# Rows normalised on GpSimd by adding a negated mean, and an instruction emitter with other costs and settings

## The chip, the cores and the metric

The kernel runs on one core of a Trainium2 chip. The metric is the device time of one execution in microseconds. The engines are named as in the profile: PE (TensorE matmul) and PEld (its weight loads), DVE (VectorE), ACT (ScalarE), POOL (GpSimd) and SP (SyncE, which here only issues transfers).

## What is computed

Two transformer layers on x of 2048 rows by 512 columns, in bfloat16. Each layer is attention with 32 heads of width 16, and a gated feed-forward part with 1792 hidden columns. Cut to what matters:

```python
def _A_ref(x, wqkv, wo):
    q, k, v = split(x @ wqkv)                       # 32 heads of 16 columns
    scores = jnp.einsum("bhqd,bhkd->bhqk", q, k) * (Dh ** -0.5)
    p = _softmax(scores, axis=-1)
    o = jnp.einsum("bhqk,bhkd->bhqd", p, v)
    return o_as_rows @ wo

def _B_ref(x, w_gate, w_up, w_down):
    return (_gelu(x @ w_gate) * (x @ w_up)) @ w_down

x = x + _A_ref(_layernorm(x), A_wqkv, A_wo)
x = x + _B_ref(_layernorm(x), B_w_gate, B_w_up, B_w_down)
x = x + _A_ref(_layernorm(x), A_wqkv, A_wo)         # the same weights again
x = x + _B_ref(_layernorm(x), B_w_gate, B_w_up, B_w_down)
```

`_layernorm` subtracts the mean of a row and divides by the root of its variance plus 1e-5.

## The kernel before

The work that takes the time is the exponential of the scores: 2 layers x 32 heads x 2048 x 2048. A tile is 128 keys by 512 queries of one head. Four heads make a group and lie 32 partitions apart; eight groups and four blocks of 512 queries make 32 units a layer, each of 64 tiles, so there are 4096 tiles. For each tile PE multiplies keys by queries (line 1392), an engine takes the exponential, and PE multiplies the result with V (line 1538); V has a column of ones, which gives the row sums as well. Products with V of four heads run side by side in PE.

Two engines share the exponentials. ScalarE takes groups of three and of two PSUM banks in turn, one instruction for each (line 1406), and writes fPT. VectorE takes single tiles by another way: it turns scores into the bits of a float16 by adding a bias and storing as int16 (line 1446, into fPI), and then makes three shifted copies of up to four such tiles at once (line 1486, into fPP), so that a sum of four approximations is taken. Each VectorE tile thus needs four products with V, where one of ScalarE needs one.

The order of all instructions is fixed before the kernel runs, by an emitter inside the kernel's own Python. It keeps a modelled clock for each engine. Every instruction has a written cost, and `_Sched.op` places it where its engine and its inputs are free by that clock. The main loop at the end of `_emit_fast` asks, at each moment that PE is free in the model: are banks free for the next scores (`fill`)? If not, is there time before they are for products with V (`pv`), for a piece of the feed-forward part or a projection (`Piece`), or for filler[...] (`keep_clock`, line 1558, a product with zeros)? VectorE, GpSimd and transfer jobs are taken from queues by `pump_one`, by modelled start time and priority. On the chip each engine runs its own list in that order, held by semaphores alone: where a written cost is wrong, an engine waits in front of an instruction that the model thought ready.

`vector_tile` decides whether the next slot of scores brings a tile for VectorE. It adds up the modelled work that stands before VectorE and says yes while this is less than `DVE_LATE`. `behind` and `pace` hold VectorE tiles back while a feed-forward part lags.

After attention on a block of queries, `post` runs its output projection (line 640 with fWO), adds x (line 1055), and normalises the rows in `ln_thread`: statistics on VectorE (lines 587 and 588), for two rows of tiles at a time the factor on GpSimd in `ln_scale` (lines 594 and 596), the rows themselves in `ln_apply` (line 606), and a transposing transfer (`turn`, line 288) into fXNT. Then come the gate and up products (line 1070) and the down products (line 1134). A row of tiles is normalised on GpSimd in all blocks but the last of a layer, 36 in all; the others go to VectorE. `ln_apply` with `eng` "pool" and with `eng` "dve" is the same instruction before the change: subtract the mean, multiply by the factor.

The very last block is cut into two halves of 256 queries, so that little is left after the last exponential.

Of the kernel before, what the change touches and what calls it, by code (L numbers as in the profile page):

```python
# [11 lines left out]
ALU = mybir.AluOpType  # L12
ACTF = mybir.ActivationFunctionType
AX = mybir.AxisListType
AP = bass.AP
# [160 lines left out]
def _emit_fast(nc, es, x_in, wqkv, wo, wg, wu, wd, out, n_rep=2):  # L176
# [10 lines left out]
    F = wg.shape[1]  # L187
# [10 lines left out]
    VW = 17  # L198
    NPH = 4
    NPART = 6  # L200
    DVE_LATE = 2.0
    WAIT_D = 0.45
    OCT = 1024.0
    LOG2E = 1.4426950408889634
# [23 lines left out]
    CM05 = sb("fCM05", [128, 4], F32)  # L228
    QMASK = sb("fQMASK", [128, 2], F32)
    ZV = sb("fZV", [128, VW], F16)  # L230
    NPT = 7
    PT = sb("fPT", [128, NPT, 1536], BF)
# [5 lines left out]
    Q = sb("fQ", [128, NQS, 512], F16)  # L238
# [21 lines left out]
    sch = _Sched()  # L260
# [22 lines left out]
    def turn(grp, dst, src, r, w):  # L283
        if grp not in sch.groups:
            sch.add_dma_group(grp, serial=True)
        t = max(sch.free["sp"], sch.ready("sp", r, w)) + 1.0
        wire[0] = max(t, wire[0]) + 128 / 180.0
        return sch.op("sp", lambda e: e.dma_start_transpose(dst, src), r=r, w=w, grp=grp, cost=1.0,
                      lat=wire[0] - t + 1.6)

    SW, MM = 0.107, 0.216
    HAM, LEAST, BACK = 3.413, 0.425, 0.425
# [8 lines left out]
    def change(kind):  # L301
        return SW if kind_now[0] != kind else 0.0
# [164 lines left out]
    def job(eng, prio, ops, then=None, ported=False):  # L467

        serial[0] += 1
        jobs[eng].append((prio, serial[0], ops, then, ported or eng == "pool"))  # L470
# [109 lines left out]
    def xn(i, alt):  # L580
        return HT[:, i + 4 * alt, 0:D].bitcast(F16)
# [5 lines left out]
        dve(prio, [(lambda e: e.bn_stats(ST[:, i, :], rows), [key], [("ST", i)], 0.72),  # L587
                   (lambda e: e.bn_aggr(MV[:, i, :], ST[:, i, :]), [("ST", i)], [("MV", i)], 0.1)], then)

    def ln_scale(n, then, lo=0):  # L590
        keys = [("MV", lo + i) for i in range(n)]
        var = AP(MV, 2 * lo + 1, [[16, 128], [2, n]])
        job("pool", 1, [
            (lambda e: e.tensor_scalar(LNS[:, 0, lo:lo + n], var, LN_EPS, None, op0=ALU.add), keys,
             [("LNS", lo + i) for i in range(n)], 0.25),
            (lambda e: e.tensor_tensor(LNS[:, 1, lo:lo + n], LNS[:, 0, lo:lo + n], CM05[:, 0:n], op=ALU.pow),
             [("LNS", lo + i) for i in range(n)] + [("CM05",)], [("LNS", lo + i) for i in range(n)], 0.45 + 0.16 * n)], then)

    def ln_check(n, lo=0):
        var = AP(MV, 2 * lo + 1, [[16, 128], [2, n]])  # L600
# [1 line left out]
                 [("MV", lo + i) for i in range(n)] + [("OKV",)], [("OKV",)], 0.1)])  # L602

    def ln_apply(i, rows, key, eng, alt, then=None, us=None, st=0):
        us = us or (1.05 if eng == "pool" else 0.46)
        job(eng, 1, [(lambda e: e.tensor_scalar(xn(i, alt), rows, MV[:, st + i, 0:1], LNS[:, 1, st + i:st + i + 1],  # L606
                                                op0=ALU.subtract, op1=ALU.mult),
                      [key, ("LNS", st + i), ("MV", st + i)], [xnkey(i, alt)], us)], then, ported=True)

    def transpose_piece(i, tt, alt=False, eng="dve", then=None):  # L610
# [65 lines left out]
    def qproj(layer, up):  # L676

        qb, c = min(up // NCK, NQB - 1), up % NCK
        h = up // NCK - (NQB - 1) if layer == n_rep - 1 and NQB > 1 and up // NCK >= NQB - 1 else None
        q0, qn = (0, 512) if h is None else (256 * h, 256)  # L680

        def evac(b):
            ops = []
            for p in range(2):
                slot = (layer * NU + 2 * up + p) % NQS
                ops.append((lambda e, p=p, slot=slot: e.tensor_scalar(Q[:, slot, q0:q0 + qn], bank(b)[:, 0:qn],
                                                                     QMASK[:, p:p + 1], None, op0=ALU.mult),
                            [BK[b], ("QMASK",)], [("Q", slot)], 0.086 + 0.001042 * qn))
            evac_job(1, b, ops, got((layer, "q", up)))
        lo = 512 * qb + q0  # L690
        return mm_piece([(WQ[:, ck, 128 * c:128 * (c + 1)], XNT[:, ck, lo:lo + qn]) for ck in range(NCK)],
                        [("XNT", t) for t in range(lo // 128, (lo + qn) // 128)] + [("WQ", c)], evac, cols=qn)
# [312 lines left out]
    def ln_thread(tts, xsl, check, name, eng, step=2):  # L1005

        nt = len(tts)
        by_dma = step != 1

        def applied(i):  # L1010
            def then(o):
                have.add(("xn", name, i))
                if by_dma:
                    transpose_by_dma(i, tts[i], got(("tr", name, i)))
            return then

        def scale(lo):
            hi = min(lo + step, nt)

            def apply(o):  # L1020
                for i in range(lo, hi):
                    ln_apply(i, X[:, xsl[i], :], ("X", xsl[i]), eng, False, applied(i))
            ln_scale(hi - lo, apply, lo)
            if check:
                ln_check(hi - lo, lo)

        ready = 0
        for i, tt in enumerate(tts):
            while ("xn", name, i) not in have:
                while ready < nt and all(("st", name, k) in have for k in range(ready, min(ready + step, nt))):  # L1030
                    scale(ready)
                    ready += step
                yield None
            if not by_dma:
                yield transpose_piece(i, tt, eng="act" if step == 1 and i % 2 == 0 else "dve", then=got(("tr", name, i)))
        while not all(("tr", name, i) in have for i in range(len(tts))):
            yield None
# [336 lines left out]
    def a_slot(atiles, dtile):  # L1374
# [24 lines left out]
        for x in both:  # L1399
            for k in tile_keys(x):  # L1400
                if k not in keys:
# [3 lines left out]
        bks = [BK[b] for b in banks[:na]]  # L1405
        o = sch.op("act", lambda e: e.activation(PT[:, p, 0:512 * na].rearrange("p (a b) -> p a b", a=na),  # L1406
                                                 PS[:, b0:b0 + na, :], ACTF.Exp, scale=1.0 / (OCT * LOG2E)),
                   r=bks, w=[("PT", p)], cost=0.049 + 0.427 * na + (1.3 if table["gelu"] else 0), lat=0.16)
        table["gelu"] = False

        def add(x, t, rhs, rk, buf):
# [253 lines left out]
    while True:  # L1665
        t = now[0] = max(now[0], sch.free["pe"])
        pump(t)
        feed_shifts()
        while closing and (closing[0][2] == "B" or os_free):
            evac(*closing.pop(0))  # L1670
        pump(t)
        if not left() and not returned[0] and ("gelu", n_rep - 1, NQB - 1, 1 if NQB > 1 else None) in have \
                and not any(slot_open):
            returned[0] = True
            free_banks.update(range(5))
        if posts_done[0] == total_posts and not any(jobs.values()):
            break
        if gelu_q and sch.ready("act", [("HT", i) for i in range(NFT)]) <= max(t, sch.free["act"]):
            gelus(*gelu_q.pop(0))
        F = fill_ready()  # L1680
        if F is not None and F <= t + 0.02:
            fill()
            continue
        limit = 99.0
        stuck[0] = F is None and not (pend.get(("PT", pt_no[0] % NPT)) and left())
        if F is not None:
            limit = max(F, sch.free["act"] - 0.44) - t
        its = pv_ready(t)
        byj = [sum(1 for it in its if it[1] == j) for j in range(4)]
        fit = int((limit - change("col")) / MM + 0.3)  # L1690
        full = min(byj)
        rest = False
        if its:
            uk = unit_order[0]
            rest = uk in closed and unit_left[uk] == 0 and len(its) == len(unit_q[uk])
            if rest:
                full = max(byj)
        press = F is None and left() and pend.get(("PT", pt_no[0] % NPT)) or shifts and pend.get(("PP", shifts[0][0]))
        if press and its:
            full = max(full, 1)  # L1700
        want = 1 if pend.get(("PI", dg["n"] % NPI)) and not dg["items"] else 3
        if fit >= 1 and (full >= want or full and (rest or press)):
            pv(its, min(fit, full, 6))
            continue
        cand = None
        for src in sources:
            p = src.peek()
            if p is None:
                continue
            bs = piece_banks(p)  # L1710
            if bs is None or piece_ready(p, bs) > t + 0.02 or p.cost + change("full") > limit + max(p.tol, src.tol()):
                continue
            cand = (src, p, bs)
            break
        if cand:
            src, p, bs = cand
            src.piece = None
            emit_piece(p, bs)
            continue
        if full and fit >= 1:  # L1720
            pv(its, min(fit, full))
            continue
        if acc["free"] and not over[0] and density(t) < DENSE and (F is None or F - t >= change("col") + MM) \
                and sch.ready("pe", [("ZV",), ("ONB",)], [BK[ACC]]) <= t:
            keep_clock()
            log["warm"] += 1
            continue
        now[0] = t + 0.05
        log["idle"] += 0.05
        assert now[0] < 20000.0, "no progress"  # L1730
# [859 lines left out]
```

## Time and profile before

| | us |
|---|---|
| time, median of 3 (lowest, highest) | 1654.21 (1649.93, 1656.24) |
| span of the profiled execution | 1652.7 |
| ScalarE: exponentials, 1296 instructions | 1481.1 |
| VectorE: tiles, 858 instructions of line 1446 | 582.8 |
| VectorE: shifted copies, 726 instructions of line 1486 | 443.7 |
| GpSimd: normalised rows, 36 instructions of line 606 | 81.7 |

A row of the groups in the profile gives line, engine, operation, what it writes and reads, the shape and the count; then the busy time in us and the mean of one in ns; then the idle time of the engine just before these instructions and what ended most of it. Instructions that overlap on an engine count once in busy time, so a mean of one can be more than busy time divided by the count. Code lines are those of the kernel before.

### The profile page before, as it was taken

To read this page: it belongs to the slowest core of one execution; us is meant where nothing else is said; L and a number is where in the kernel's file an instruction comes from. 1 tells how busy PE (TensorE), PEld (TensorE's weight loads), DVE (VectorE), ACT (ScalarE), POOL (GpSimd) and SP (SyncE) were. 2 spreads that over 40 slices of the span, in tenths; PEclk is the share of its full clock that TensorE was granted. 3 is DMA by queue.
4 is the path that set the end of the run, shared out by engine and by line. 5 is a ranking of instruction groups with operands and counts; after the bars stand their busy time and mean duration, and the time that the engine had idled before them with its cause. 6 is when DMAs were issued, how large, how long until landed. Compare 5 with 4: busy or idle time off the path is not lost.

```text
span 1652.7 us, 38882 instructions
## 1 busy us (share of the span) xinstructions
PE 1556.2 (94%) x16505; PEld 515.0 (31%) x16505; DVE 1366.5 (83%) x2339; ACT 1556.9 (94%) x1340; POOL 218.1 (13%) x201
## 2 busy tenths in 40 slices
PE   8999989998999999999999989999999999999998
PEld 3332222222222222332332322222222222444455
DVE  7999998889978899887643899888898889887873
ACT  6999999999999999999999999999999999999991
POOL 2420020003200222002510100200030000300000
PEclk9999999999999999999999999999999999999999
DMA  5200111115121421113323111221411114122343
GB/s 147 59 5 8 48 35 53 49 49 118 38 61 34 105 69 37 52 33 93 80 66 114 36 45 34 65 56 31 127 31 45 53 38 107 39 60 66 86 134 95
DMA packets 162371, 103.27 MB, mean 62 GB/s; under 512 B 54928, under 2 KB 145296, under 8 KB 162192
## 3 DMA queue, kind: packets, MB, share of 16 engines
q1 hardware_dynamic: 158096, 95.98, 22.1%
q0 software_dynamic: 2112, 4.19, 0.9%
q8 instruction: 134, 2.20, 0.6%
q10 hardware_dynamic: 1984, 0.53, 0.1%
q14 instruction: 45, 0.37, 0.1%
HBM read 76.81 MB, written 15.20 MB: 56 GB/s over the span
## 4 chain that ended last, share of the span: by engine, by line
ACT 47%; PE 37%; DVE 9%; DMA 3%; POOL 3%; issue 1%; SPq 0%; POOLq 0%; DVEq 0%; ACTq 0%
ACT fPT L1406 45%; PE fPS L1538 10%; PE fPS L1392 10%; PE fPS L1070 8%; PE fPS L1134 4%; DVE fPI L1446 3%; DVE fPP L1486 3%; PE fPS L640 3%; ACT fHT L1355 2%; POOL fHT L606 2%; DMA fRB<-rscr 1%; DMA fXNT<-fHT 1%; PE fPS L1558 1%; DMA rscr<-fLT 1%; ACT L1355 1%
## 5 line engine op out<-in xcount | busy, mean ns | idle before, releaser
L1406 ACT ACTIVATE fPT<-fPS 128x1536 bf16<-128x1536 f32 (+1 forms) x1296 | 1481.1, 1286 | 49.1 <-PE fPS L1392 45.0
L1446 DVE TENSOR_SCALAR fPI<-fPS 128x512 int16<-128x512 f32 x858 | 582.8, 685 | 108.5 <-PE fPS L1392 103.1
L1392 PE MATMUL fPS<-fQ,fKT 32*128 32x512 f16 (+1 forms) x4608 | 520.1, 360 | 57.7 <-ACT fPT L1406 39.6
L1538 PE MATMUL fPS<-fPT,fVP 128*17 128x512 bf16 (+1 forms) x3640 | 470.6, 359 | 6.6 <-DVE fOS L944 2.6
L1486 DVE TENSOR_SCALAR fPP<-fPI 128x2048 int16<-128x2048 int16 (+3 forms) x726 | 443.7, 642 | 8.8 <-PE fPS L1538 3.4
L1538 PE MATMUL fPS<-fPP,fVD 128*17 128x512 f16 (+1 forms) x2904 | 416.4, 358 | 3.6 <-DVE fPP L1486 1.7
L1392 PEld LDWEIGHTS fPS<-fQ,fKT 32*128 32x128 f16 x4608 | 142.3, 91 | 541.3 <-ACT fPT L1406 403.5
L1538 PE MATMUL fPS<-fPI,fVP 128*17 128x512 f16 (+1 forms) x968 | 259.0, 357 | 1.3 <-DVE fOS L944 0.7
L1070 PE MATMUL fPS<-fXNT,fWR 128*128 128x512 f16 (+1 forms) x952 | 220.0, 363 | 12.0 <-DVE fHT L1113 5.5
L909 POOL TENSOR_TENSOR fAT<-fOP,fRB 128x512 f16<-128x512 f32 (+1 forms) x36 | 42.2, 1173 | 1100.0 <-DMA fRB<-rscr 1100.0
L1538 PEld LDWEIGHTS fPS<-fPT,fVP 128*17 128x17 f16 x3640 | 118.5, 88 | 155.2 <-issue 97.2
L1558 PE MATMUL fPS<-fONB,fZV 128*17 128x512 f16 x1944 | 151.7, 385 | 1.7 <-POOL fQMASK L372 1.5
L1538 PEld LDWEIGHTS fPS<-fPP,fVD 128*17 128x17 f16 x2904 | 113.0, 89 | 108.8 <-issue 52.7
L1134 PE MATMUL fPS<-fWR,fHT 128*128 128x512 bf16 x428 | 120.5, 383 | 0.6 <-DVE fX L1165 0.2
L1113 DVE TENSOR_TENSOR fHT<-fPS,fHT 128x512 bf16<-128x512 f32 x112 | 76.1, 688 | 50.2 <-PE fPS L1070 31.6
L1070 PEld LDWEIGHTS fPS<-fXNT,fWR 128*128 128x128 bf16 x952 | 77.3, 98 | 119.1 <-DVE fPI L1446 22.3
L1089 DVE CAST fHT<-fPS 128x512 bf16<-128x512 f32 x105 | 71.8, 687 | 32.4 <-PE fPS L1070 32.2
L606 POOL TENSOR_SCALAR fHT<-fX,fMV,fLNS 128x512 f16<-128x512 f32 x36 | 81.7, 2276 | 3.2 <-PE fPS L1134 1.3
L1538 PEld LDWEIGHTS fPS<-fPI,fVP 128*17 128x17 f16 x968 | 65.5, 88 | 31.6 <-issue 16.5
L720 POOL TENSOR_SCALAR fVD<-fVP 128x544 f16<-128x544 f16 (+1 forms) x48 | 54.6, 1138 | 102.0 <-DVE fVP L728 99.3
L1558 PEld LDWEIGHTS fPS<-fONB,fZV 128*17 128x17 f16 x1944 | 45.0, 90 | 48.3 <-issue 22.5
L944 DVE COPY fOS<-fPS 128x512 f32<-128x512 f32 (+1 forms) x72 | 44.8, 623 | 13.1 <-PE fPS L1538 12.4
(68 smaller groups left out, 609.6 us busy)
## 6 DMA issues: line engine op xcount, KB each, us to landing
fWR<-in_B_w_up_dram SPq DMA_DIRECT2D x62, 256.0 KB, 2.9
fWR<-in_B_w_down_dram SPq DMA_DIRECT2D x58, 256.0 KB, 2.8
fWR<-in_B_w_gate_dram SPq DMA_DIRECT2D x57, 256.0 KB, 4.9
oscr<-fOS SPq DMA_DIRECT2D x224, 32.0 KB, 1.7
fOP<-oscr SPq DMA_DIRECT2D x28, 256.0 KB, 2.7
fRB<-rscr SPq DMA_DIRECT2D x28, 256.0 KB
fX<-in_A_x_dram POOLq DMA_DIRECT2D x4, 1024.0 KB, 5.6
xscr<-fX SPq DMA_DIRECT2D x16, 256.0 KB, 2.8
```

The costliest lines, as they stand in the source:

```text
L606: job(eng, 1, [(lambda e: e.tensor_scalar(xn(i, alt), rows, MV[:, st + i, 0:1], LNS[:, 1, st + i:st + i + 1], op0=ALU.subtract, op1=ALU.mult),
L720: job("pool", 2, [(lambda e, dst=dst, src=src, ph=ph: e.tensor_scalar(dst, src, 2.0 ** (-ph / NPH), None, op0=ALU.mult), [("VP", c, k) for ...
L1070: ins = e.matmul(bank(bs[0])[:, w * qn:(w + 1) * qn], lhsT=wchunk(s, (ft + w) % 2, ck), rhs=XNT[:, ck, xs], start=(ck == 0), stop=(ck == N ...
L1089: evac_job(1, b, [(lambda e: e.tensor_copy(in_ht(ft), in_bank(b)), [BK[b]], fk, 0.6)], got(("gate", layer, qb, h, ft)))
L1113: (lambda e: e.tensor_tensor(in_ht(ft), in_bank(b), in_ht(ft), op=ALU.mult), [BK[b]] + fk, fk, 0.62)], got(("up", layer, qb, h, ft))))
L1134: ins = e.matmul(bank(b)[:, 0:D], lhsT=HT[:, ft, i * 128:(i + 1) * 128], rhs=wslot(s)[:, jj * D:(jj + 1) * D], start=(ft == 0), stop=(ft = ...
L1392: ins = e.matmul(bank(b)[:, b0:b0 + qn], lhsT=KT[32 * j:32 * j + 32, (x[1] % NG) // 2, kt * 128:(kt + 1) * 128], rhs=Q[32 * j:32 * j + 32, ...
L1406: o = sch.op("act", lambda e: e.activation(PT[:, p, 0:512 * na].rearrange("p (a b) -> p a b", a=na), PS[:, b0:b0 + na, :], ACTF.Exp, scale ...
L1446: dve(0, [(lambda e: e.tensor_scalar(PI[:, gi, 512 * r:512 * (r + 1)], bank(bd), DBIAS, 0.0, op0=ALU.add, op1=ALU.max), [BK[bd]], [("PI", ...
L1486: shifts.append((s, [(lambda e: e.tensor_scalar(PP[:, s, 0:512 * n], PI[:, gi, 0:512 * n], int(OCT) * ph // NPH, None, op0=ALU.add), [("PI ...
L1538: ins = e.matmul(PS[32 * j:32 * j + VW, ACC, 0:qn], lhsT=l, rhs=r_, start=a, stop=z, tile_position=(0, 32 * j), skip_group_check=True)
L1558: ins = e.matmul(PS[32 * j:32 * j + VW, ACC, :], lhsT=ZV[:, :], rhs=ones, start=False, stop=False, tile_position=(0, 32 * j), skip_group_c ...
```

## The change

It does three things.

1. A row normalised on GpSimd no longer subtracts its mean. `ln_scale` makes the negated mean with one more small GpSimd instruction where the rows go to GpSimd, and `ln_apply` adds it. Rows on VectorE stay as they were.
2. The emitter's model gets other costs for a transposing transfer (`turn`), a row on GpSimd, the evacuation of queries, and an exponential.
3. Settings of the emitter change: `DVE_LATE` from 2.0 to 2.82, and two small constants by which the main loop decides how many products with V fit before the next scores.

Points 2 and 3 change no instruction by themselves. They change the order of instructions on all engines, and the split of the tiles between ScalarE and VectorE.

```diff
-    DVE_LATE = 2.0
+    DVE_LATE = 2.82
...
     def turn(grp, dst, src, r, w):
-        t = max(sch.free["sp"], sch.ready("sp", r, w)) + 1.0
+        t = max(sch.free["sp"], sch.ready("sp", r, w)) + 1.2
         wire[0] = max(t, wire[0]) + 128 / 180.0
-        return sch.op("sp", lambda e: e.dma_start_transpose(dst, src), r=r, w=w, grp=grp, cost=1.0,
-                      lat=wire[0] - t + 1.6)
+        return sch.op("sp", lambda e: e.dma_start_transpose(dst, src), r=r, w=w, grp=grp, cost=1.2,
+                      lat=wire[0] - t + 0.6)
...
-    def ln_scale(n, then, lo=0):
+    def ln_scale(n, then, lo=0, on="dve"):
         keys = [("MV", lo + i) for i in range(n)]
+        mean = AP(MV, 2 * lo, [[16, 128], [2, n]])
...
+            (lambda e: e.tensor_scalar(LNS[:, 2, lo:lo + n], mean, -1.0, None, op0=ALU.mult),
+             keys + [("LNS", lo + i) for i in range(n)], [("LNS", lo + i) for i in range(n)], 0.25)][:3 if on == "pool" else 2], then)
...
-        us = us or (1.05 if eng == "pool" else 0.46)
-        job(eng, 1, [(lambda e: e.tensor_scalar(xn(i, alt), rows, MV[:, st + i, 0:1], LNS[:, 1, st + i:st + i + 1],
-                                                op0=ALU.subtract, op1=ALU.mult),
+        us = us or (0.8 if eng == "pool" else 0.46)
+        by, how = (LNS[:, 2, st + i:st + i + 1], ALU.add) if eng == "pool" else (MV[:, st + i, 0:1], ALU.subtract)
+        job(eng, 1, [(lambda e: e.tensor_scalar(xn(i, alt), rows, by, LNS[:, 1, st + i:st + i + 1], op0=how, op1=ALU.mult),
...
-                            [BK[b], ("QMASK",)], [("Q", slot)], 0.086 + 0.001042 * qn))
+                            [BK[b], ("QMASK",)], [("Q", slot)], 0.126 + 0.001042 * qn))
...
-            ln_scale(hi - lo, apply, lo)
+            ln_scale(hi - lo, apply, lo, eng)
...
-                   r=bks, w=[("PT", p)], cost=0.049 + 0.427 * na + (1.3 if table["gelu"] else 0), lat=0.16)
+                   r=bks, w=[("PT", p)], cost=0.062 + 0.427 * na + (1.3 if table["gelu"] else 0), lat=0.16)
...
-            limit = max(F, sch.free["act"] - 0.44) - t
+            limit = max(F, sch.free["act"] - 0.437) - t
...
-        fit = int((limit - change("col")) / MM + 0.3)
+        fit = int((limit - change("col")) / MM + 0.29)
```

More of the change, by code (lines that the diff above doesn't have):

```diff
@@ L596, in ln_scale @@
             (lambda e: e.tensor_tensor(LNS[:, 1, lo:lo + n], LNS[:, 0, lo:lo + n], CM05[:, 0:n], op=ALU.pow),
-             [("LNS", lo + i) for i in range(n)] + [("CM05",)], [("LNS", lo + i) for i in range(n)], 0.45 + 0.16 * n)], then)
+             [("LNS", lo + i) for i in range(n)] + [("CM05",)], [("LNS", lo + i) for i in range(n)], 0.45 + 0.16 * n),
+            (lambda e: e.tensor_scalar(LNS[:, 2, lo:lo + n], mean, -1.0, None, op0=ALU.mult),
+             keys + [("LNS", lo + i) for i in range(n)], [("LNS", lo + i) for i in range(n)], 0.25)][:3 if on == "pool" else 2], then)
     def ln_check(n, lo=0):
```

## The prediction

> **What bounds the kernel now.** I read the page's busy table first, then the chain of waits, then the groups with their shapes kept apart, then stretches of 50 us, and last the waits.
>
> ```profile
> PE 1556.2 (94%) x16505; PEld 515.0 (31%) x16505; DVE 1366.5 (83%) x2339; ACT 1556.9 (94%) x1340; POOL 218.1 (13%) x201
> ...
> ACT 47%; PE 37%; DVE 9%; DMA 3%; POOL 3%; issue 1%; SPq 0%; POOLq 0%; DVEq 0%; ACTq 0%
> ```
>
> PE and ScalarE show the same 94%. The next rows part them.
>
> ```profile
> L1406 ACT ACTIVATE fPT<-fPS 128x1536 bf16<-128x1536 f32 x647 | 969.4, 1498 | 40.3 <-PE fPS L1392 36.7
> L1406 ACT ACTIVATE fPT<-fPS 128x1024 bf16<-128x1024 f32 x648 | 696.4, 1075 | 8.8 <-PE fPS L1392 8.3
> L1446 DVE TENSOR_SCALAR fPI<-fPS 128x512 int16<-128x512 f32 x858 | 582.8, 685 | 108.5 <-PE fPS L1392 103.1
> L1486 DVE TENSOR_SCALAR fPP<-fPI 128x2048 int16<-128x2048 int16 x549 | 370.9, 705 | 5.1 <-PE fPS L1538 0.7
> L1558 PE MATMUL fPS<-fONB,fZV 128*17 128x512 f16 x1944 | 151.7, 385 | 1.7 <-POOL fQMASK L372 1.5
> L606 POOL TENSOR_SCALAR fHT<-fX,fMV,fLNS 128x512 f16<-128x512 f32 x36 | 81.7, 2276 | 3.2 <-PE fPS L1134 1.3
> ```
>
> L1558 multiplies zeros to keep PE's clock up: PE's 94% holds 151.7 us of filler. ScalarE has none. The exponentials were idle for 49.1 us before them in all (40.3 + 8.8), nearly all waits for L1392, the scores; 4.8 us of that is the first one. Stretch by stretch (columns: us, then busy PE, PEld, DVE, ACT, POOL, then clock and DMA):
>
> ```profile
> 50.00:100.00 50.00, 47.92 (x523) 17.91 (x519) 46.23 (x78) 50.00 (x45) 13.63 (x13) 1.00 0.09 22
> ...
> 850.00:900.00 50.00, 48.58 (x345) 15.37 (x343) 17.32 (x28) 48.82 (x39) 0.94 (x2) 1.00 0.27 80
> ...
> 950.00:1000.00 50.00, 44.84 (x537) 12.28 (x538) 47.47 (x79) 50.00 (x45) 3.82 (x3) 1.00 0.20 51
> ```
>
> From the first exponential at 16.3 us to the last one's end at 1609.7 us **ScalarE sets the pace**, at 50.00 of 50 in many stretches. VectorE is close behind in pure attention (46 to 47.5) and has room in the blocks with gate and up products. The last 43 us, with no exponential, are a chain of normalisation, transfers and PE products.
>
> **What the skill says.** "Perfetto Trace Analysis", section Identifying the Most-Contended Engine, takes occupancy for ScalarE and VectorE, but not for PE, as closeness to the limit; the filler agrees. "ScalarE: Activation LUTs", section What ACT_TABLE_LOAD costs, gives 0.833 ns an element, 427 ns for 512. The trace agrees: 1498 - 1075 = 423 ns for a third bank. "GPSIMD Engine Reference", section 3.1, measured 769 ns for 512 elements in a tight loop and 4497 ns for a 2048-element two-input add, a quarter of which is 1124. The trace before shows no add form of the row; its subtract form takes 2276 ns. The same page's section 8 says GpSimd shares its SBUF interfaces with VectorE; the trace has the same row at 2072 ns at least and 3027 at most, which fits.
>
> **The change, part by part.**
>
> *Where the tiles go.* The built order of instructions has 901 tiles on VectorE (L1446) instead of 858; the threshold 2.82 lets the emitter give VectorE one while 2.82 us of work stand before it, not 2.0. The 4096 tiles are fixed, so ScalarE has 3195 instead of 3238, in 1279 exponentials instead of 1296. From 901.64 us the chain holds 108 exponentials in 122.27 us, 1.132 us each; at 2.5 tiles that is 2.5 x 0.423 + 0.075. Saved: 43 x 0.423 + 17 x 0.075 = 18.2 + 1.3 = **19.5 us of ScalarE, on the path**.
>
> *What VectorE pays.* 43 more L1446, and in L1486 39 more of width 2048, 6 fewer of 1536, 3 more of 1024, 15 fewer of 512. By durations 43 x 0.685 + 39 x 0.705 - 6 x 0.563 + 3 x 0.427 - 15 x 0.294 = 29.5 + 21.0 = 50.5 us. The union of busy time would be 1417, 87% of the new span. Packed, L1446 starts follow each other at 0.606 us in the trace, so some 45 us really. Idle time before L1446, 108.5 us, is what hides it. Of the 43, about 9 fall before the first projection and 7 in the stretch from 901 to 1030 us, where VectorE was busy 115.8 of 129: 7 tiles at 1.2 us are 8.2 us, while ScalarE gives back 7 x 0.45 = 3.2: 115.8 + 8.2 = 124.0 of 125.8. It fits narrowly. I charge **+3 us** for PE waiting on VectorE there.
>
> *PE.* Four products with V replace one per moved tile: 147 calls more in the built order, with some of half width. In the chain 12 such calls take 0.22 us more than 8, so a round of four is 0.22 us and the whole 147 / 4 x 0.22 = 8 us. Filler falls from 486 rounds of four to 423, 63 x 0.22 = 14 us. Cost nothing: the filler given up hides it.
>
> *The row on GpSimd.* 36 rows, two pairs in each of nine normalisations. A new 128x2 multiply before each pair, 18 at 0.29 us. The add is between 0.77 us (the page's loop) and 2.28 us (no gain). I take 0.8 to 1.1. The two-input multiply of the same size on GpSimd, L909, took 1289 ns in this trace, so 2276 for a row with one tensor input is out of line, and a form without the subtraction should stay under L909. A pair then ends 2 x 1.3 - 0.3 = 2.3 us sooner. Behind the pair stand the transposes, then the first gate product, then the next scores on PE's queue, for which ScalarE waits. This is that chain in the first block:
>
> ```profile
> 237.39 4.68 POOL fHT L606 x2
> 242.06 0.02 issue
> 242.08 3.32 DMA fXNT<-fHT
> 245.40 0.14 issue
> 245.54 0.59 PE fPS L1070 x2
> ```
>
> ScalarE's gaps behind such handoffs are 1.91, 1.00, 0.99, 0.42 and 1.16 us: 5.5 in all. Three of the nine normalisations have a reader far away (the next layer's keys). The emitter also puts the gate earlier, since it now believes 0.8 rather than 1.05, and a landing sooner: the transpose issues at 1.198 us and lands 2.5 us after issue, by the trace; the old model said 1.0 + 0.71 + 1.6 = 3.3, the new one 1.2 + 0.71 + 0.6 = 2.5. Both edits go to the measured values. So only half of the gaps is recovered: **-2.5 us**.
>
> *The exponential's cost* goes from 0.049 to 0.062: a pair of 3 and 2 tiles from 2.233 to 2.259 us against 2.264 measured. No work changes; PE's cushion before ScalarE shrinks by up to 1279 x 0.013 = 17 us over the run. Bounds: nothing, or a part of that as new gaps; I count it with the +3 above. Q's evacuation and the last two constants (0.437, 0.29) are under 0.05 us each, within the order's noise.
>
> *The end.* The built order now puts all 28 down products of the first half block after the last scores; of 172 filler products ahead of the last projection 32 stay. The final 28 down products took 6.16 us in the chain, and with 8 rounds of filler at 0.22 that makes 8 us, inside the 10.1 us that PE has from the last product with V (1611.9) to the projection at 1622.0. Cost: nothing; the transfers of the row sums hide it.
>
> Sum: -19.5 + 3 - 2.5 = -19.0. From 1654.2: **1635 us**.
>
> **The rivals.** *Half eaten.* Added VectorE backlog (0.82 us more) delays evacuations, and PE in order passes this to ScalarE. For it: the 124.0 of 125.8 above; against it: no gap in 124.8 to 245 us, where VectorE is over 90%. Ten us lost: 1645. *The add is no faster.* Then each handoff is late by 2 x (2.28 - 0.8) = 3.0 instead of 2 x (2.28 - 1.05) - 0.8 = 1.7 us: nine times 1.3 is 12 us, 1654.2 - 19.5 + 12 = 1647. *VectorE becomes the bound.* If two thirds of the 50.5 us cannot be hidden, 34 - 19.5 = +14.5: 1669, slower. Idle of 108.5 us before L1446 speaks against it. *All waits recovered.* All 5.5 us of gaps go, and half of the 12.5 us that ScalarE waits for scores from 1400 to 1610 us: 1654.2 - 19.5 - 5.5 - 6 = 1623.
>
> **How the numbers follow.** Forecast 0.60; half eaten 0.12; add no faster 0.08; VectorE bound 0.08; all recovered 0.12. The range leaves out VectorE bound and small ends of others: 1621 to 1650. Half a per cent is 8.3 us, 1645.9. Faster: 0.60 + 0.12 + most of half eaten 0.08 + 0.02 = 0.82; same 0.10; slower 0.08.
>
> **What would show it.** Right: 1279 exponentials, ScalarE busy near 1537; L1446 x901 and DVE near 1410; the GpSimd row at 0.8 to 1.1 us; the exponentials' idle still near 49; the last 43 us unchanged. Wrong: idle before the exponentials over 65 us, with PE's scores waiting for L1446 or L1486; a GpSimd row over 2 us with L1070 waiting for transposes; a tail longer than 46 us.

## The result, and the profile after

The changed kernel takes 1626.49 us (1625.13 to 1629.08, 4 runs) beside 1654.27 for the kernel before: a ratio of 0.9837, 95% interval 0.9814 to 0.9861. That is 27.8 us less, where 19.0 were forecast. The range held it and the direction was right; the gain was half as large again as the sum of its terms.

Code lines after the change stand three or four higher: the exponential is L1409, VectorE's tile L1449, its shifted copies L1489, the scores L1395, products with V L1541, filler L1561, VectorE's copy of the results of attention L947, the GELU L1358, GpSimd's scaling by the row sums L912, the normalised row L610, the gate and up products L1073. First the busy table and the chain's shares of the changed kernel, in the same order as before:

```profile
PE 1546.1 (95%) x16400; PEld 509.6 (31%) x16400; DVE 1393.4 (86%) x2403; ACT 1542.8 (95%) x1323; POOL 175.6 (11%) x219
...
PE 42%; ACT 34%; DVE 18%; DMA 3%; issue 1%; POOL 1%; SPq 0%; DVEq 0%; POOLq 0%; ACTq 0%
```

The groups with shapes kept apart (busy us, mean ns of one, then idle time before them and its end):

```profile
L1409 ACT ACTIVATE fPT<-fPS 128x1536 bf16<-128x1536 f32 x638 | 941.9, 1476 | 32.1 <-PE fPS L1395 28.2
L1409 ACT ACTIVATE fPT<-fPS 128x1024 bf16<-128x1024 f32 x640 | 673.3, 1052 | 6.7 <-PE fPS L1395 5.1
L1449 DVE TENSOR_SCALAR fPI<-fPS 128x512 int16<-128x512 f32 x901 | 610.1, 685 | 72.1 <-PE fPS L1395 67.5
L1489 DVE TENSOR_SCALAR fPP<-fPI 128x2048 int16<-128x2048 int16 x588 | 399.5, 701 | 4.2 <-PE fPS L1541 1.4
L610 POOL TENSOR_SCALAR fHT<-fX,fLNS 128x512 f16<-128x512 f32 x36 | 32.5, 911 | 2.0 <-POOL fLNS L599 0.4 <-PE fPS L1395 0.2
```

There are three things to see. The exponentials are fewer, as the built order said. Their idle time is 38.8 us instead of 49.1, so waits have gone too, where the forecast had them nearly even. And the GpSimd row takes 911 ns in the mean instead of 2276. Two of the stretches shown before, again as us, then busy PE, PEld, DVE, ACT and POOL:

```profile
50.00:100.00 50.00, 46.75 (x531) 16.16 (x528) 47.67 (x79) 49.72 (x45) 12.63 (x9) 1.00 0.05 10
...
950.00:1000.00 50.00, 46.92 (x547) 12.81 (x543) 49.22 (x84) 49.44 (x44) 3.90 (x3) 1.00 0.15 43
```

From 950 us VectorE is now busy for 49.22 of 50 (47.47 before). ScalarE, at 49.44, no longer leaves it behind: in pure attention the two are balanced, and the chain of waits passes through VectorE for 18% of the span instead of 9%.

The span splits in three: the head up to the first exponential, the middle, and the tail from the last exponential's end. The last end is found from ScalarE's next activation less the idle time before it: 1627.17 - 17.45 = 1609.7 before, 1600.13 - 15.76 = 1584.4 after.

| us | before | after | difference |
|---|---|---|---|
| head | 16.3 | 14.7 | -1.6 |
| middle | 1593.4 | 1569.7 | -23.7 |
| tail | 43.0 | 41.2 | -1.8 |
| span | 1652.7 | 1625.6 | -27.1 |

The head is the same work, and in twelve other profiles of variants it lies between 14.0 and 15.7 us, so I read nothing into it. The middle has two parts. Packed starts of exponentials lie 1.330 us apart for three banks and 0.904 for two (medians, alike in both traces): 9 and 8 fewer are 12.0 + 7.2 = 19.2 us. The other 4.5 us of the middle are waits, as ScalarE's other work there takes 67.7 us in both. That is less than the 10.3 us by which the idle time fell: an exponential is recorded as some 0.15 us longer than its packed step, so a delay shorter than that leaves no idle time in the profile. Below I give both: the idle time, and the change of the middle less that of the packed steps.

### The profile page after: what moved, and what is told of

Its sections match the earlier page's. It is cut to its first block, busy times and chain, and to the rows that moved or that the text cites. A ratio compares the mean times of both kernels' runs of the same rounds, so it can differ in the third digit from the quotient of the medians.

```text
span 1625.6 us, 38751 instructions
## 1 busy us (share of the span) xinstructions
PE 1546.1 (95%) x16400; PEld 509.6 (31%) x16400; DVE 1393.4 (86%) x2403; ACT 1542.8 (95%) x1323; POOL 175.6 (11%) x219
## 4 chain that ended last, share of the span: by engine, by line
PE 42%; ACT 34%; DVE 18%; DMA 3%; issue 1%; POOL 1%; SPq 0%; DVEq 0%; POOLq 0%; ACTq 0%
ACT fPT L1409 32%; PE fPS L1541 12%; PE fPS L1395 12%; PE fPS L1073 9%; DVE fPI L1449 8%; DVE fPP L1489 6%; PE fPS L1137 4%; PE fPS L643 3%; ACT fHT L1358 2%; DMA fRB<-rscr 2%; PE fPS L1561 1%; DMA rscr<-fLT 1%; DVE fQ L689 1%; DVE fHT L1092 1%; DVE fOS L947 1%
## 5 line engine op out<-in xcount | busy, mean ns | idle before, releaser
L1409 ACT ACTIVATE fPT<-fPS 128x1536 bf16<-128x1536 f32 x1279 | 1466.9, 1263 | 38.8 <-PE fPS L1395 33.3
L1449 DVE TENSOR_SCALAR fPI<-fPS 128x512 int16<-128x512 f32 x901 | 610.1, 685 | 72.1 <-PE fPS L1395 67.5
L1395 PE MATMUL fPS<-fQ,fKT 32*128 32x512 f16 (+1 forms) x4608 | 514.9, 360 | 42.4 <-ACT fPT L1409 27.4
L1489 DVE TENSOR_SCALAR fPP<-fPI 128x2048 int16<-128x2048 int16 (+3 forms) x747 | 467.7, 649 | 10.0 <-PE fPS L1541 6.3
L1541 PE MATMUL fPS<-fPT,fVP 128*17 128x512 bf16 (+1 forms) x3591 | 462.9, 359 | 6.0 <-DVE fOS L947 3.0
L1541 PE MATMUL fPS<-fPP,fVD 128*17 128x512 f16 (+1 forms) x3051 | 426.0, 357 | 4.8 <-DVE fPP L1489 2.6
L1395 PEld LDWEIGHTS fPS<-fQ,fKT 32*128 32x128 f16 x4608 | 139.2, 91 | 514.9 <-ACT fPT L1409 356.9
L1541 PE MATMUL fPS<-fPI,fVP 128*17 128x512 f16 (+1 forms) x1017 | 268.4, 359 | 2.8 <-DVE fOS L947 1.4
L1073 PE MATMUL fPS<-fXNT,fWR 128*128 128x512 f16 (+1 forms) x952 | 219.7, 362 | 8.9 <-DVE fHT L1116 4.2
L1541 PEld LDWEIGHTS fPS<-fPT,fVP 128*17 128x17 f16 x3591 | 117.5, 88 | 149.8 <-issue 89.7
L912 POOL TENSOR_TENSOR fAT<-fOP,fRB 128x512 f16<-128x512 f32 (+1 forms) x36 | 43.8, 1216 | 1055.1 <-DMA fRB<-rscr 1027.6
L1541 PEld LDWEIGHTS fPS<-fPP,fVD 128*17 128x17 f16 x3051 | 114.8, 89 | 118.6 <-issue 51.0
L1561 PE MATMUL fPS<-fONB,fZV 128*17 128x512 f16 x1692 | 141.4, 390 | 1.7 <-POOL fQMASK L372 1.5
L1073 PEld LDWEIGHTS fPS<-fXNT,fWR 128*128 128x128 bf16 x952 | 76.8, 97 | 116.3 <-DVE fPI L1449 27.1
L1116 DVE TENSOR_TENSOR fHT<-fPS,fHT 128x512 bf16<-128x512 f32 x112 | 76.3, 689 | 41.2 <-PE fPS L1073 29.7
L1541 PEld LDWEIGHTS fPS<-fPI,fVP 128*17 128x17 f16 x1017 | 68.3, 89 | 42.9 <-issue 18.1
L947 DVE COPY fOS<-fPS 128x512 f32<-128x512 f32 (+1 forms) x72 | 45.0, 625 | 14.3 <-PE fPS L1541 13.6
L1561 PEld LDWEIGHTS fPS<-fONB,fZV 128*17 128x17 f16 x1692 | 39.3, 91 | 42.6 <-issue 25.1
L689 DVE TENSOR_SCALAR fQ<-fPS,fQMASK 128x512 f16<-128x512 f32 (+1 forms) x72 | 46.1, 683 | 2.9 <-PE fPS L643 2.9
```

Source lines behind the costliest of these rows:

```text
L947: fn = lambda e: e.tensor_copy(OS[:, s, 0:qn], bank(ACC)[:, 0:qn])
L1073: ins = e.matmul(bank(bs[0])[:, w * qn:(w + 1) * qn], lhsT=wchunk(s, (ft + w) % 2, ck), rhs=XNT[:, ck, xs], start=(ck == 0), stop=(ck == N ...
L1116: (lambda e: e.tensor_tensor(in_ht(ft), in_bank(b), in_ht(ft), op=ALU.mult), [BK[b]] + fk, fk, 0.62)], got(("up", layer, qb, h, ft))))
L1395: ins = e.matmul(bank(b)[:, b0:b0 + qn], lhsT=KT[32 * j:32 * j + 32, (x[1] % NG) // 2, kt * 128:(kt + 1) * 128], rhs=Q[32 * j:32 * j + 32, ...
L1449: dve(0, [(lambda e: e.tensor_scalar(PI[:, gi, 512 * r:512 * (r + 1)], bank(bd), DBIAS, 0.0, op0=ALU.add, op1=ALU.max), [BK[bd]], [("PI", ...
L1489: shifts.append((s, [(lambda e: e.tensor_scalar(PP[:, s, 0:512 * n], PI[:, gi, 0:512 * n], int(OCT) * ph // NPH, None, op0=ALU.add), [("PI ...
```

## The experiments

All ratios are against the kernel before.

**One: the add form alone.** The edit to the kernel before; the small multiply is given a modelled cost that leaves the emitter's clock, and so the order of everything else, as it was.

```diff
+            (lambda e: e.tensor_scalar(LNS[:, 2, lo:lo + n], mean, -1.0, None, op0=ALU.mult), ... -0.15)
-        ... rows, MV[:, st + i, 0:1], LNS[:, 1, ...], op0=ALU.subtract, op1=ALU.mult
+        by, how = (LNS[:, 2, ...], ALU.add) if eng == "pool" else (MV[:, ...], ALU.subtract)
```

> The kernel before with the GpSimd rows in the add form and nothing else: costs, settings and the order of all other instructions are those of before (858 tiles on VectorE, 1296 exponentials); only the negated mean stands in between. Theory tiles (the time follows the tiles moved off ScalarE): only the gaps behind the GpSimd rows can go, 5.5 us at most, so 1649 to 1654, ratio 0.997 to 1.000. Rival rows (the faster row gives most of the gain): 1640 or less, ratio under 0.992. In both the row itself takes near 0.8 to 0.9 us.

Measured: 1645.37 us, ratio 0.9945 (0.9929 to 0.9960), 8.8 us less. Both theories missed; the row is worth more than the gaps I had counted and less than most of the gain. The row and the first handoff in this kernel's trace:

```profile
L610 POOL TENSOR_SCALAR fHT<-fX,fLNS 128x512 f16<-128x512 f32 x36 | 28.4, 796 | 2.1 <-POOL fLNS L599 0.4 <-PE fPS L1137 0.2
```

```profile
235.61 1.54 POOL L610 TENSOR_SCALAR fHT<-fX,fLNS 128x512 f16<-128x512 f32 x2
...
242.28 1.04 PE L1073 MATMUL fPS<-fXNT,fWR 128*128 128x512 f16 x4
...
243.70 2.37 ACT L1409 ACTIVATE fPT<-fPS 128x1536 bf16<-128x1536 f32 x2 [0.36 <-PE fPS L1395]
```

A pair of rows takes 1.54 us where it took 4.68; the gate product no longer waits for the transpose, and ScalarE's gap of 1.91 us is 0.36. Over the run the idle time before the exponentials falls from 49.1 to 41.1 us, 8.0 of the 8.8, and the middle is 7.3 us shorter with the same exponentials.

**Two: the threshold alone.**

```diff
-    DVE_LATE = 2.0
+    DVE_LATE = 2.82
```

> The kernel before with the threshold 2.82 instead of 2.0 and nothing else: 896 tiles on VectorE, 1281 exponentials. Theory tiles: 38 tiles at 0.426 us and 15 exponentials at 0.05 us less on ScalarE are 16.9 us: 1637, ratio 0.990. Rival VectorE full (the added 38 tiles make PE wait for VectorE): half or more of it is eaten, 1646 or more. Rival model (the mended costs are what makes the new threshold pay): 1650 or more.

Measured: 1637.37 us, ratio 0.9896 (0.9880 to 0.9912), 16.8 us less, close to the 16.9 of the count of tiles. The exponentials of this kernel:

```profile
L1406 ACT ACTIVATE fPT<-fPS 128x1536 bf16<-128x1536 f32 (+1 forms) x1281 | 1467.1, 1273 | 49.7 <-PE fPS L1392 45.3
```

Idle time is 49.7, against 49.1 before. That 38 more tiles on VectorE cost ScalarE nothing is not shown by it: the middle of this profile is 1580.8 us, 12.6 less than before, where 8 exponentials of three banks and 7 of two fewer are 17.0 us of packed steps. Some 4.4 us of waits came in, and a head and a tail shorter by 1.9 and 1.6 us made up for most of them. This is one trace each, and four runs of the kernel before lie between 1649.9 and 1656.2 us, so the 4.4 us are not clear of the scatter.

**Three: the new order with the slow row.** The kernel after, with the subtraction back in the instruction only; the model still reckons with 0.8 us.

```diff
-        by, how = (LNS[:, 2, st + i:st + i + 1], ALU.add) if eng == "pool" else ...
+        by, how = (MV[:, st + i, 0:1], ALU.subtract) if eng == "pool" else ...
```

> The kernel after with the order unchanged, but the GpSimd rows subtract the mean again (the small multiply stays, its result unused). Theory handoff (an order that reckons with 0.8 us a row needs the faster row): each of six handoffs to a gate late by 2 to 3 us, 12 to 18 us: 1638 to 1645. Rival slack (the rows lie beside other work): 1626 to 1630.

Measured: 1641.94 us, ratio 0.9934 (0.9916 to 0.9952), 15.5 us more than after. Two lines show the row and who pays: the group, and from the view of waits PE's gate products behind the transposes (total us, times, longest).

```profile
L610 POOL TENSOR_SCALAR fHT<-fX,fMV,fLNS 128x512 f16<-128x512 f32 x36 | 85.8, 2390 | 2.0 <-POOL fLNS L599 0.4 <-PE fPS L1395 0.2
```

```profile
PE fPS L1073 <- DMA fXNT<-fHT: 9.6, 7, 2.7
```

After the change that wait was 0.8 us. ScalarE has gaps of 1.24, 1.99, 4.12, 3.03 and 1.24 us behind five of the six handoffs, and one of 2.52 us at 788 us behind rows for the next layer's keys, whose reader the prediction had taken for far away. The idle time before the exponentials is 54.0 us, 15.2 more than after. The handoff theory holds: an order that believes in 0.8 us needs the fast row.

**Four: the new row and costs with the old threshold.**

```diff
-    DVE_LATE = 2.82
+    DVE_LATE = 2.0
```

> The kernel after with the threshold back at 2.0: 872 tiles on VectorE, 1290 exponentials, so 14 tiles and 6 exponentials less on ScalarE than before, 6.3 us. Theory tiles plus some 8 us of smaller waits from the new row and the mended costs: 1640, ratio 0.991. If the row and the mended costs do nothing: 1648. If they are most of the gain: 1633 or less.

Measured: 1646.16 us, ratio 0.9950 (0.9936 to 0.9963). All three guesses missed, the nearest by 2 us. It has 14 tiles fewer on ScalarE than experiment one, worth 6.3 us, and is no faster. Its profile says where they went: the middle is 1584.2 us, only 1.9 less than in experiment one, so 4.4 us of the 6.3 went into waits there, which no run explains; and the tail is 45.8 us, not 42.6. The end of its chain of waits, and from the view in order of time GpSimd's scaling by the row sums, the last thing that the projection needs:

```profile
1600.72 2.70 PE fPS L1137 x12
1603.41 10.90 PE fPS L1561 x200
1614.32 0.16 issue
1614.47 0.82 PE fPS L643 x3
```

```profile
1613.14 0.73 POOL L912 TENSOR_TENSOR fAT<-fOP,fRB 128x256 f16<-128x256 f32 x1 [19.20 <-DMA fRB<-rscr]
```

The emitter put 200 filler products in front of the projection, as many as its own clock for the transfers asked for. On PE they run in order, and the projection stands behind them: here **the filler is what ends the wait**. But it does so by little: the scaling ended at 1613.87 us, and the projection began 0.6 us later. The scaling itself ended 13.1 us after the last product with V, where it takes 9.6 us in the changed kernel, because the transfers of the row sums took longer. Why they did is open. That filler could end the wait was not expected, and the next runs follow it.

**Five: add form and threshold together, with the old costs and constants.** Edits one and two.

> The kernel before with the add form and the threshold 2.82 together, but the old costs and constants; the order is that of the threshold alone (896 tiles, 1281 exponentials). Theory sum: the two parts measured singly add, 1654.2 - 8.8 - 16.8 = 1628.6, ratio 0.9845, so that the mended costs are worth 2 us at most. Rival overlap (both draw on the same idle time of ScalarE): 1633 or more. Rival costs (the mended costs carry a part): 1633 or more as well; the idle before the exponentials tells them apart: over 45 us for overlap, under 40 with a longer tail for costs.

Measured: 1628.41 us, ratio 0.9854 (0.9829 to 0.9879). The sum holds to 0.2 us, and the idle time before the exponentials is 38.7 us, the same as after. Between it and experiment one the threshold shortens the middle by 16.4 us, 0.6 less than its packed steps. What this leaves to the mended costs and the last two constants is 1.9 us, within the intervals of both.

**Six to eight and eleven: thresholds, costs and constants around the changed kernel.** Each is the kernel after with one edit:

```diff
# six
-    DVE_LATE = 2.82
+    DVE_LATE = 3.6
# seven: cost of an exponential
-cost=0.062 + 0.427 * na
+cost=0.049 + 0.427 * na
# eight
-            limit = max(F, sch.free["act"] - 0.437) - t
+            limit = max(F, sch.free["act"] - 0.44) - t
-        fit = int((limit - change("col")) / MM + 0.29)
+        fit = int((limit - change("col")) / MM + 0.3)
# eleven: the transposing transfer
-cost=1.2, lat=wire[0] - t + 0.6
+cost=1.0, lat=wire[0] - t + 1.6
```

> The kernel after with the threshold 3.6: 917 tiles on VectorE, 1272 exponentials. Theory tiles: 16 tiles and 7 exponentials less than after, 7.2 us: 1619. Rival VectorE full: its idle before the tiles was 72 us after the change; another 16 tiles at 1.08 us fill 17 of it and PE waits more: half eaten 1623, all eaten 1626 or more, with more idle before the exponentials.

> The kernel after with the exponential's old cost, 0.049 instead of 0.062: 902 tiles, 1278 exponentials, another order. Theory split: the same number of tiles gives the same time, 1626, give or take 3 for the order. Rival cushion (the higher cost lets PE run ahead less tightly and helps ScalarE): 1632 or more. Rival exact (packed starts lie 0.904 and 1.330 us apart, which is the old cost): 1623 or less.

> The kernel after with the last two constants back at 0.44 and 0.3: the same 901 tiles and 1279 exponentials, another order. It shows what the order alone does: theory split 1626.5, give or take 3. Rival order (the two constants were worth much): 1632 or more.

> The kernel after with the old cost of a transposing transfer: 902 tiles, 1279 exponentials, 9.0 us of PE work between the last product with V and the projection. Theory split and tail: 1626, give or take 3, tail 41. Rival costs (the mended landing lets the gate products come at the right time): 1632 or more, idle before the exponentials 45 or more.

Measured: six 1636.12 us (0.9885, 0.9863 to 0.9906), seven 1636.97 (0.9896, 0.9876 to 0.9916), eight 1628.18 (0.9848, 0.9828 to 0.9869), eleven 1624.69 (0.9835, 0.9814 to 0.9855). Eight and eleven are the same as after: neither the two constants nor the mended transfer is worth anything that can be told. Seven has the split of after and is 10 us slower. Its tail is 48.6 us, 7.4 longer, and the middle is 3.8 us longer although ScalarE has 5.8 us less to do in it (61.9 us besides exponentials, not 67.7): the last GELU has moved into the tail. The idle time before the exponentials is 50.6 us, 11.8 more than after, with one gap of 7.98 us before an exponential at 800 us: there the chain runs through seven transfers on SyncE's queue, with the last transpose of a block issued behind the others, and keys' products and scores wait for it. So the time is that of the rival with the cushion, 1632 or more, but the profile puts most of the loss at two places of a slower order, and not at many small waits. Whether the cost of an exponential matters as such stays open. Six has 7.2 us less for ScalarE to do and is 9.6 us slower: idle before the exponentials is 50.8 us, 12 more than after, and the tail is 45.1 us, with a transfer of the row sums that took 6.14 us there and 3.84 in after.

**Nine: nearly the same threshold, another tail.** The kernel after with 2.9. The order was chosen for what it puts in front of the last projection.

```diff
-    DVE_LATE = 2.82
+    DVE_LATE = 2.9
```

> The kernel after with the threshold 2.9 instead of 2.82: 903 tiles, 1278 exponentials, almost the same split, but an order that puts 48 up products, 28 down products and 84 filler products between the last product with V and the last block's projection: at the prices of the traces (0.115, 0.22 and 0.055 us) 17.0 us of PE work where after has 7.9. The transfers of the row sums hide 10 us of it. Theory tail: 7 us longer from the last exponential to the end, 48 us, and 1632 in all. Theory split alone: 1625, tail 41.

Measured: 1631.90 us, ratio 0.9876 (0.9856 to 0.9896), the tail 1629.4 - 1579.8 = 49.6 us. Both numbers of the tail theory are met. Its chain in the tail, cut to its first and last pieces:

```profile
1580.73 5.34 PE fPS L1073 x48
...
1594.61 3.56 PE fPS L1137 x16
1598.17 0.76 PE fPS L1561 x12
1598.92 0.98 PE fPS L643 x4
```

From 1580.7 to 1598.9 us PE never waits: up products, filler and down products stand in front of the projection. The scaling by the row sums was late here too. These lines of the view in order of time, from three engines, show why:

```profile
1581.10 1.70 ACT L1358 ACTIVATE fHT<-fHT 128x1792 bf16<-128x1792 bf16 x1
...
1582.83 3.68 DVE L1116 TENSOR_TENSOR fHT<-fPS,fHT 128x512 bf16<-128x512 f32 x6 [1.62 <-ACT fHT L1358]
1586.42 0.19 DVE L871 RECIPROCAL fLT<-fLT 128x8 f32<-128x8 f32 x1
...
1594.84 0.73 POOL L912 TENSOR_TENSOR fAT<-fOP,fRB 128x256 f16<-128x256 f32 x1 [11.27 <-DMA fRB<-rscr]
```

The last GELU runs after the last exponential at 1579.8 us, and VectorE's multiplication of the up products with the gate (L1116) waits for it, and the reciprocal of the row sums stands behind six of these on VectorE. The scaling ended at 1595.57 us, and PE held the projection for another 3.3 us. In the changed kernel the GELU ended before the last exponential, and the same place looks like this:

```profile
1584.57 0.78 PE fPS L1541 x20
...
1585.83 2.11 DMA fLT<-fOS
...
1588.20 1.96 DMA rscr<-fLT
...
1590.23 3.84 DMA fRB<-rscr
...
1594.20 0.73 POOL fAT L912
...
1594.98 1.05 PE fPS L643 x4
```

There the transfers end last, and PE's 8 us lie beside them. Set side by side, with PE's products between the two at 0.115 us for an up product, 0.22 for a down product and 0.055 for a filler product, and with times counted from the end of the last product with V:

| kernel | PE work in front of the projection, us | scaling ended, us | projection begins, us | tail, us |
|---|---|---|---|---|
| after | 7.9 | 9.6 | 9.7 | 41.2 |
| eleven | 9.0 | 9.0 | 9.6 | 41.4 |
| before | 9.9 | 10.1 | 10.1 | 43.0 |
| four | 13.6 | 13.1 | 13.8 | 45.8 |
| seven | 14.0 | 12.8 | 14.9 | 48.6 |
| nine | 17.0 | 14.8 | 18.1 | 49.6 |
| six | 8.1 | 11.9 | 12.0 | 45.1 |

Nine has 96 filler products there, not the 84 of its expectation, whose sum of 17.0 holds with 96. In every row the projection begins when the later of the two is done. In four, seven and nine PE's work is, by 0.6, 2.0 and 3.3 us: only that much of the longer tails is PE's alone, as the scaling came later there as well. In six the slow transfer holds the projection, and PE's work does not. Nor is a longer tail all loss: in seven and nine the middle is relieved of the 5.8 us of ScalarE's work for the last GELU. Nine's tail is 8.5 us longer than after's, but its span only 3.9 us, as its middle is 4.3 us shorter. The theory had counted on the same middle, so that its 1632 was met in part by luck.

**Ten and twelve: the backlog.** The kernel after with the threshold 4.5, and the kernel before with the add form and 3.6 (old costs).

> The kernel after with the threshold 4.5: 917 tiles and 1272 exponentials as with 3.6, in another order, with 8.1 us of PE work between the last product with V and the projection (that of 3.6 has the same). Theory tiles: 1619, if what 3.6 lost was the luck of its order. Theory backlog (more work standing before VectorE delays evacuations that PE waits for): 1630 or more, with 45 us or more of idle time before the exponentials and a tail near 41 to 45.

> The kernel before with the add form and the threshold 3.6, old costs: 909 tiles, 1275 exponentials, 9.0 us of PE work between the last product with V and the projection. Theory tiles: 13 tiles and 6 exponentials less than with 2.82, 5.8 us: 1623. Theory backlog: 1628 or more, with more idle before the exponentials than the 39 us that add form and 2.82 had.

Measured: ten 1636.21 us (0.9899, 0.9880 to 0.9918) with a tail of 40.7, twelve 1630.11 us (0.9863, 0.9842 to 0.9883) with a tail of 41.5. Their exponentials, ten first; the rows are from two kernels:

```profile
L1409 ACT ACTIVATE fPT<-fPS 128x1536 bf16<-128x1536 f32 x1272 | 1460.6, 1265 | 55.2 <-PE fPS L1395 48.6
```

```profile
L1409 ACT ACTIVATE fPT<-fPS 128x1536 bf16<-128x1536 f32 x1275 | 1460.5, 1272 | 48.0 <-PE fPS L1395 43.2
```

With good tails and fewer exponentials ten is 9.7 us slower than after, and twelve does not gain on five (0.9863 against 0.9854, within the intervals of both), where 5.8 us were to be had. The idle time before the exponentials grows, 38.8 to 55.2 us with the new costs and 38.7 to 48.0 with the old ones. Over the whole run VectorE is not out of time, as its idle time before the tiles stays where it was (72.1 in after, 75.1, 73.7 and 79.1 in six, ten and twelve). But that is an average. In pure attention from 910 to 1010 us the stretch of after, and below it that of six, read:

```profile
910.00:1010.00 100.00, 93.73 (x1079) 27.51 (x1079) 98.30 (x167) 99.33 (x89) 10.56 (x13) 1.00 0.13 34
910.00:1010.00 100.00, 90.85 (x1024) 26.88 (x1025) 98.73 (x168) 96.45 (x86) 10.08 (x13) 1.00 0.12 29
```

VectorE has 98.3 and 98.7 us of work in 100, and ScalarE falls from 99.3 to 96.5. So "VectorE full" falls for the run as a whole, and stays possible in such stretches. That results come later because more work stands ahead of them fits as well: PE and its weight loads wait for VectorE 226 us in all in after, 240 and 253 in six and ten. In twelve it is 215, and 222 in five, which does not fit. What lengthens the gaps there stays open.

## Why the prediction was right, point by point

- *Tiles, -19.5 us.* Right. Packed starts give 19.2. The threshold alone gave 16.8 where 38 tiles and 15 exponentials come to 16.9. The fixed part of an exponential was put at 0.075 us from a chain that held small waits; packed it is 1.330 - 3 x 0.426 = 0.052, where 0.426 is the difference of the two packed steps.
- *The row on GpSimd, -2.5 us.* The mechanism was right, the size was not: alone it gave 8.8 us, and 8.0 of idle time. Two steps failed. I listed five gaps, 5.5 us; the sixth handoff to a gate, late in the run, had two more, 1.20 and 1.09 us at 1436 to 1439 us, which makes 7.8. And I halved the sum (half of 5.5 is 2.75, put down as 2.5) because the emitter puts the gate earlier once it believes in 0.8 us. It does, but the row then takes 0.77 us in most cases and 0.91 in the mean, so the gate finds its rows: the gap after the first handoff is 0.35 us in after. The 769 ns that the Trainium skill's "GPSIMD Engine Reference" gives in section 3.1 for its best loop was the right end of my bound: the fastest row after the change took 762 ns.
- *VectorE in the full stretches, +3 us.* Not settled. The idle time shows no such loss at 2.82 (49.1 to 49.7 us in experiment two, 41.1 to 38.7 from one to five). By the middle and its packed steps the waits grew by 4.4 us in the first pair and by 0.6 in the second, and of the 7.3 us that the row alone took from them the changed kernel keeps 4.5. The arithmetic of the stretch (124.0 of 125.8) was near: from 901 to 1030 us VectorE is busy for 125.6 of 129 after the change. For the run as a whole durations were added where instructions overlap: VectorE's busy time rose by 26.9 us, not 50.5. At 3.6 and 4.5 waits do come.
- *The exponential's cost.* I held 0.062 to be the measured value, 2.259 against 2.264 a pair. Packed, a pair is 2.234, which the old cost (2.233) had met. The 2.264 had waits in it. No experiment shows the cost itself as gain or loss.
- *The end.* Right: hidden in the changed kernel, and the tail 1.8 us shorter. That it would be so in any order was luck: in four, seven and nine PE's work held the projection for 0.6 to 3.3 us.
- *The signs.* Exponentials, the row and the tail came as listed. The idle time before the exponentials was to stay near 49 us and fell to 38.8, and VectorE was to be busy near 1410 us and was for 1393.4.
- *The rivals.* "All waits recovered", 1623, is 3.5 us off and came nearer than the forecast, which is 8.5 us off. It took 11.5 us from the waits, and the idle time fell by 10.3, though the waits of the middle by 4.5 only: on the gaps behind the rows it was the better account. "The add is no faster", put at 1647, was run as experiment three at 1641.9. VectorE as the bound of the run is refuted at this threshold.

The sum of what was measured singly, 8.8 + 16.8 = 25.6, leaves 2.2 us for costs, constants and order together. The 8.8 us that the forecast was short by are, by these times, the row's 6.3 and VectorE's 3, less half a us of small change. By the parts of the profile the waits of the middle went down by 4.5 us where the two terms together had them up by half a us, and head and tail, put at nothing, gave 3.4; the head's part is within the scatter of the variants.

## What to carry to other kernels

A wait behind a slow instruction on an idle engine is counted by listing every gap that it causes, over the whole run, before any of them is discounted; the engine's low share of busy time (13% before the change) does not show it. In a kernel whose order is written ahead, filler and low-priority work queued in front of the last dependent product are part of the critical path as soon as they outlast what they were meant to cover: add up the PE time between the last input and that product, and hold it against the transfers. In nine this was 3.3 us of a delay, and the same work on VectorE made the transfers start later too. And moving work to a second engine pays at the price of the first one's packed starts until idle time before the first one grows; here no threshold above 2.82 was faster, and 3.6 and 4.5 with the new costs were slower, though with fewer exponentials.

## What had not been expected of the hardware

On GpSimd the row of 128 x 512 float32 takes 2.07 to 3.56 us when it subtracts a per-row value and multiplies (before, two and three), and 0.76 to 1.82 us, most often 0.77, when it adds one and multiplies. The mean of the add form lay between 0.80 and 1.02 us in the runs that had it. The add form also takes its value from another tile, fLNS in place of fMV; no run changes the one without the other, so that the operation alone makes the difference is not shown. Exponentials out of PSUM follow each other at 0.904 us for 1024 and 1.330 for 1536 columns while each is recorded as some 1.05 and 1.48 us long, so durations overstate what one of them costs by about 0.15 us.
